# Five early weight tiles through PSUM banks, twelve instead of sixteen before the first block, and new nominal times for the planner of a fused attention and two-block MLP kernel

## The chip, the cores and the metric

The kernel runs on one core of a Trainium2 chip. The metric is device microseconds of one execution, taken as the median of several executions; less is better.

## The reference

Attention over 2 x 8 heads of 1152 keys, in which neighbouring pairs of queries are averaged first (576 pooled queries a head), then two MLP blocks over the 1152 resulting rows of 512. All arrays are float32.

```python
q_pool = q.reshape(B, H, S // 2, 2, D).mean(axis=3)        # B 2, H 8, S 1152, D 64
scores = np.matmul(q_pool, k.transpose(0, 1, 3, 2)) / np.sqrt(D)
attn = softmax(scores, axis=-1)
x = (attn @ v).transpose(0, 2, 1, 3).reshape(1152, 512)
h = x @ w_in                                               # 512 x 2048, first block
P = a[0] + a[1] * h + a[2] * h**2 + a[3] * h**3
Q = 1.0 + abs(b[0]) * abs(h) + abs(b[1]) * h**2
x = (P / (Q + 1e-06)) @ w_out                              # 2048 x 512
h = x @ w2_in                                              # second block
out = (np.maximum(h, 0) + np.log1p(np.exp(-np.abs(h)))) @ w2_out
```

## The kernel before

The two weight pairs of the MLP arrive as float64 bits. Each of the 64 weight tiles (128 x 512) is loaded as pairs of 32-bit words (`w_load`, a DMA of 512 KB on SP's queue into one of two buffers `wraw`) and decoded on the chip in five steps. In the attention part these are operations of their own, `w0` to `w4`: `w0` on ScalarE scales the high word into the tile `pk` (`w_abs`, L446), `w1` on VectorE shifts it left by three (`w_conv`, L452), `w2` on VectorE ors in bits of the low word (L458), `w3` on ScalarE copies it as the high half of the weight tile `w` (L954 in the attention part, L468 in the blocks), and `w4` on VectorE subtracts to get the low half (L396, `w<-pk,w`). `wl` is the load. In the second half of the work one more VectorE operation (L455) sets the sign. Products are made of high and low halves, three matmuls each.

The attention works through 8 pairs of heads (NP = 8; j = 0 to 7), each in 9 steps of query tiles by three column groups. A group's scores (L543, TensorE) go into a PSUM bank, VectorE takes the maximum (L550), ScalarE the exponential (L563, tile `p`), TensorE transposes (L514, tile `t`, another bank), ScalarE or GpSimd writes the rounded half (`ph`, L506, L613 and L623), VectorE or GpSimd the remainder (`pl`, L396), and TensorE multiplies by v (L643). Eight banks (NB = 8) serve all of these in turn; VectorE's and ScalarE's reads free them. The next pair's keys and queries are loaded, transposed, split (`khi`, `klo`, `qhi`, `qlo`; L783, L811, L816) and moved by DMAs on SP's queue (`dma_k`, `dma_q`, `dma_qd`, all L517) while a pair is worked. `dma_qd` copies parts of `qhi` and `qlo` into `qdh` and `qdl` (kind `dd`); `qhi` has one buffer, so the next pair's `qhi` (kind `qh0`) can't be written before those copies have read it.

The order of the whole attention part is written by a planner. Every operation has a kind and a nominal time: its base (nine units a pair) plus an offset of its kind from the table `O`, and corrections by step in the pair (`OT`) and for the first and last pair (`OJ`, `OU`). `op` adds these up; `run` sorts each engine's operations by nominal time and then issues them, always taking the engine whose head is ready first by a small model of durations. That fixes the instruction order of every engine and which bank each operation gets. `weight` makes the six operations of a weight tile.

Before the first block 16 tiles are decoded: three singly in pairs 2, 3 and 4 (NE = 3, pool `we`), and 13 around the last pair, into the space of two pools that are released then (`early` becomes `wra`, seven tiles; `even` becomes `wrb`, seven tiles).

The first block takes 48 units (24 groups of two, k = 0 to 23) of 24 matmuls up (L1054) and 24 down (L1103) for each pair of units; the activation takes 3 + 3 VectorE operations and one for the low half on 128 x 768 tiles in each group (L1077 to L1079, L1088 to L1090, L396). The remaining weight tiles are decoded meanwhile by `w_step`, which moves up to one tile each through split, convert, scale and load. `w_pace` calls it in every second unit at first (r0 = 50), later in two of five (r1 = 40), and `w_need` calls it as often as needed when a tile is wanted that isn't there. The tiles' order of use is `order`: index 0 to 15 for the first half of the first block, 16 to 31 for its second half, 32 to 63 for the second block. The second block (up L1135, down L1157) has 48 units too, with a step in nine of ten (r2 = 90), each issued after the unit's last ScalarE copy.

Of the kernel before, what the change touches and what calls it, by code (L numbers as in the profile page):

```python
# [10 lines left out]
I32 = mybir.dt.int32  # L11
# [22 lines left out]
    ne=3,  # L34
    r0=50,
    r1=40,
    r2=90,
    whd=0,
# [27 lines left out]
    "R": 2.6459,
    "U": 2.3672,
    "U1": 2.601,
    "U2": 2.8694,
    "X0": 4.1997,  # L70
    "X1": 4.539,
    "kq": -3.3775,
    "lv": 1.3594,
    "pq": 0.4094,
    "qt0": 0.6348,
    "qh0": 0.9195,
    "ql0": 1.4074,
    "qt1": 1.843,
    "qh1": 1.897,
    "ql1": 2.3854,  # L80
    "dq0": 2.0734,
    "dq1": 1.6718,
    "dd": 4.2928,
    "kt0": 4.4127,
    "kh0": 4.5969,
    "kl0": 5.3629,
    "kt1": 5.1134,
    "kh1": 5.4542,
    "kl1": 5.853,
# [31 lines left out]
    "P3": 1.2299,
    "P4": 1.4149,
    "P5": 2.1976,
    "P6": 1.5711,
    "P7": 1.8637,
    "P8": 1.9534,
}
OT = {
# [35 lines left out]
}  # L164
OJ = {
    "lv": (-1.2907, 0),
    "fa": (0.1493, 0),
    "fh": (1.1474, 0),
    "fp": (-2.3014, 0),
    "fl": (-0.1074, 0),  # L170
    "v0": (-0.2845, 0),
    "vw0": (-0.0476, 0),
    "v1": (1.894, 0),
    "vw1": (2.0223, 0),
    "S0": (-0.0354, -0.1233),
# [1177 lines left out]
```

## Time and profile before

| what | value |
|---|---|
| median of 3 runs | 713.07 us (712.73 to 715.3) |
| profiled execution, its own time | 711.51 us |
| span of the profiled execution | 709.4 us |
| TensorE busy | 681.0 us (96%) |
| VectorE busy | 556.5 us (78%) |
| ScalarE busy | 493.5 us (70%) |
| GpSimd busy | 207.3 us (29%) |
| first matmul of the first block | 298.1 us |
| first matmul of the second block | 496.5 us |

The span runs from the first to the last instruction; 2.1 us of the execution lie outside it. Busy times are sums over the whole span, in which the attention and the two blocks have different limits, so the engines are compared stretch by stretch. A busy TensorE is not TensorE at its peak: ends of matmuls are modelled and small waits between them can hide.

### The profile page before, as it was taken

What the parts mean: (1) busy time and instruction counts of PE and PEld (TensorE: products, weight loads), DVE (VectorE), ACT (ScalarE), POOL (GpSimd) and SP (SyncE); (2) the same over time, 40 slices, a digit from 0 to 9 for tenths busy, and PEclk for the clock granted to TensorE, in tenths of its full rate; (3) what the DMA queues carried; (4) which work ended last, traced back from release to release, by engine and by line L of the source; (5) the groups of instructions that cost most, each with busy time, mean ns of one, the idle gap of its engine ahead of it and who ended that gap; (6) DMA issues with size and microseconds to landing.
All of it is one profiled execution on the core that took longest, in us unless ns stands there. A gap on an engine that the chain in (4) does not pass through costs nothing.

```text
span 709.4 us, 11830 instructions
## 1 busy us (share of the span) xinstructions
PE 681.0 (96%) x4076; PEld 633.2 (89%) x4076; DVE 556.5 (78%) x1080; ACT 493.5 (70%) x1135; POOL 207.3 (29%) x357
## 2 busy tenths in 40 slices
PE   7998999999999987789999999999999999999997
PEld 6898999998999875689999999999999999999996
DVE  5987989999898899989999999999775775511122
ACT  4888999989999998778777677776544554422221
POOL 4876687777768545600000000000000000000000
PEclk9999999999999999999999999999999999999999
DMA  3383736464736643431221022210043342101011
GB/s 100 102 187 85 171 90 163 114 155 104 179 84 141 148 128 120 140 98 60 62 86 62 31 84 72 83 57 3 2 149 118 95 141 92 61 1 45 1 45 44
DMA packets 60395, 65.68 MB, mean 93 GB/s; under 512 B 21552, under 2 KB 49456, under 8 KB 60336
## 3 DMA queue, kind: packets, MB, share of 16 engines
q1 hardware_dynamic: 59152, 63.95, 33.5%
q10 hardware_dynamic: 1184, 0.98, 0.4%
q8 instruction: 32, 0.52, 0.3%
q14 instruction: 27, 0.22, 0.1%
HBM read 47.71 MB, written 2.36 MB: 71 GB/s over the span
## 4 chain that ended last, share of the span: by engine, by line
PE 62%; DVE 15%; ACT 13%; DMA 4%; issue 4%; SPq 1%; ACTq 0%; DVEq 0%
PE acc L1157 14%; PE h L1135 14%; PE t L514 8%; PE pv L643 8%; PE s L543 8%; PE acc L1103 5%; PE h L1054 5%; ACT p L563 4%; DMA wraw<-in_moe_w_in_dram 3%; DVE p L1077 2%; DVE m L1089 2%; DVE m L1079 2%; ACT ph L506 2%; DVE p L1088 1%; ACT c L613 1%
## 5 line engine op out<-in xcount | busy, mean ns | idle before, releaser
L563 ACT ACTIVATE p<-s,mb 128x384 f32<-128x384 f32 x216 | 125.4, 593 | 6.1 <-DVE mb L554 5.9
L550 DVE TENSOR_REDUCE nm<-s 128x1 f32<-128x384 f32 x216 | 111.7, 550 | 12.6 <-PE s L543 11.1
L396 DVE TENSOR_TENSOR gl<-p,gh 128x384 fp32r<-128x384 f32 (+1 forms) x72 | 49.6, 690 | 91.3 <-ACT gh L1144 90.0
L514 PE MATMUL t<-ident,p 128*128 128x128 f32 x648 | 102.0, 277 | 8.4 <-ACT p L563 6.1
L1054 PE MATMUL h<-xh,w 128*128 128x384 f32 x384 | 99.4, 338 | 3.5 <-DVE p L1078 2.5
L1143 ACT ACTIVATE p<-h 128x384 f32<-128x384 f32 x48 | 23.6, 492 | 108.8 <-PE h L1135 108.7
L1135 PE MATMUL h<-xh,w 128*128 128x384 f32 x384 | 98.4, 336 | 0.0
L514 PEld LDWEIGHTS t<-ident,p 128*128 128x128 f32 x648 | 78.8, 142 | 18.8 <-ACT p L563 12.2
L1103 PE MATMUL acc<-gh,w 128*128 128x384 f32 x384 | 92.9, 336 | 0.3 <-ACT gh L1064 0.2
L643 PE MATMUL pv<-ph,v 128*128 128x256 f32 (+1 forms) x288 | 90.9, 326 | 1.0 <-ACT p L563 0.5
L1157 PE MATMUL acc<-w,gh 128*128 128x512 f32 x288 | 89.5, 392 | 0.0
L396 DVE TENSOR_TENSOR pl<-t,ph 128x384 fp32r<-128x384 f32 (+1 forms) x160 | 78.6, 510 | 4.4 <-ACT ph L506 3.7
L643 PE MATMUL pv<-pl,v 128*64 128x256 f32 (+1 forms) x288 | 78.1, 299 | 1.8 <-POOL pl L396 0.5
L396 POOL TENSOR_TENSOR pl<-c,ph 128x384 fp32r<-128x384 f32 (+1 forms) x80 | 75.8, 952 | 5.1
L506 ACT CAST ph<-t 128x384 fp32r<-128x384 f32 (+1 forms) x160 | 70.8, 467 | 5.7 <-PE t L514 4.8
L1135 PEld LDWEIGHTS h<-xh,w 128*128 128x128 f32 x384 | 70.5, 188 | 4.3 <-ACT p L1143 0.4
L1054 PEld LDWEIGHTS h<-xh,w 128*128 128x128 f32 x384 | 70.1, 190 | 4.4 <-issue 4.3
L1103 PEld LDWEIGHTS acc<-gh,w 128*128 128x128 f32 x384 | 68.6, 188 | 1.6 <-ACT gh L1064 1.5
L1054 PE MATMUL h<-xl,w 128*128 128x384 f32 x192 | 64.8, 338 | 0.0
L1135 PE MATMUL h<-xl,w 128*128 128x384 f32 x192 | 64.7, 337 | 0.0
L1157 PEld LDWEIGHTS acc<-w,gh 128*128 128x128 f32 x288 | 53.4, 188 | 9.0
L1103 PE MATMUL acc<-gl,w 128*128 128x384 f32 x192 | 59.1, 335 | 0.0
(129 smaller groups left out, 1475.4 us busy)
## 6 DMA issues: line engine op xcount, KB each, us to landing
wraw<-in_moe_w_in_dram SPq DMA_DIRECT2D x32, 512.0 KB, 3.9
wraw<-in_moe_w_out_dram SPq DMA_DIRECT2D x32, 512.0 KB, 3.3
vr<-in_v_dram SPq DMA_DIRECT2D x8, 576.0 KB, 6.2
kr<-in_k_dram SPq DMA_DIRECT2D x15, 288.0 KB, 5.1
qr<-in_q_dram SPq DMA_DIRECT2D x15, 256.0 KB, 4.4
out_dram<-m SPq DMA_DIRECT2D x15, 128.0 KB, 1.7
ks1a<-khi SPq DMA_DIRECT2D x4, 288.0 KB, 3.2
ks1a<-klo SPq DMA_DIRECT2D x4, 288.0 KB, 4.0
```

The lines of the kernel that those rows point to most:

```text
L396: return eng.tensor_tensor(out=o, in0=a, in1=b, op=ALU.subtract)
L506: nc.scalar.copy(out=out, in_=in_)
L514: nc.tensor.transpose(o[0:rows, i * 128:i * 128 + n], a, ident[0:n, 0:n])
L543: nc.tensor.matmul(out=o, lhsT=p, rhs=r, start=(m == 0), stop=(m == len(l) - 1))
L550: op("M" + str(n % 3), "DVE", fn=lambda: nc.vector.tensor_reduce(out=NM[i][:, n:n + 1], in_=tl[k], axis=AX.X, op=ALU.max, negate=True), R= ...
L563: nc.scalar.activation(out=o, in_=tl[k], func=AF.Exp, bias=MB[i][:, t:t + 1], accum_out=DEN[i][:, n:n + 1])
L643: nc.tensor.matmul(out=o, lhsT=p, rhs=r[:, m, 0:w], start=(c == a == 0), stop=(c == C - 1 and a == 1))
L1054: nc.tensor.matmul(out=h, lhsT=w[:, wi, wd], rhs=x[:, d, xcols(c)], start=(n == 0), stop=(n == 3 * ND - 1))
L1103: nc.tensor.matmul(out=st["acc", c, d], lhsT=w[:, wi, wd], rhs=g, start=(first and n == 0), stop=(last and n == 2))
L1135: nc.tensor.matmul(out=h, lhsT=w[:, wi, d * 128:(d + 1) * 128], rhs=x[:, d, xcols(c)], start=(n == 0), stop=(n == len(mm) - 1))
L1143: nc.scalar.activation(out=p, in_=h, func=AF.Softplus)
L1157: nc.tensor.matmul(out=st["acc", c, t], lhsT=g[:, t * 128:(t + 1) * 128], rhs=w[:, wi], start=(first and n == 0), stop=(last and n == 2))
```

## The change

Five tiles instead of three are decoded singly, at base times 13.8, 23.1, 30.3, 39.7 and 47.7 (pairs 1 to 5), and seven instead of 13 around the last pair, at bases 61.5 to 67.1; the list `wt` holds all twelve. `pk` of these tiles is a PSUM bank out of the planner's eight instead of a tile in SBUF, and `w1`, `w2` and `w4` no longer count in the planner's model as holders of the port that VectorE and GpSimd share. `wrb` is not filled before the first block; its seven places go to the list `freed`, with two fewer of `wl_`. The first block's steps start at tile 12, not 16, and stop for its last six units (rq = 6). The tile `p` has five buffers, not six. All nominal times are new; corrections now exist by pair (0, 6, 7) and, for the first pair's preparation and the weight tiles, by operation (`OF`). `run` may look past a blocked head when all heads are blocked.

```diff
-    ne=3,
+    ne=5,
+    wt=(13.827, 23.117, 30.255, 39.714, 47.66, 61.48, 62.487, 63.019, 64.546, 64.568, 65.923, 67.055),
+    rq=6,
...
-    "kq": -3.3775,
+    "kq": -1.7841,
-    "dd": 4.2928,
+    "dd": 3.7605,
-    "qh0": 0.9195,
+    "qh0": 0.981,
...
-    "dd": (1.5635, 0),
+    ("dd", 0): 0.106,
...
-NB, NP_, NPH, NCP = 8, 6, 5, 2
+NB, NP_, NPH, NCP = 8, 5, 5, 2
...
-        if kind in OJ and not 0 < j < 7:
-            when += OJ[kind][j >= 7]
-        if kind in OU and not 0 < j < 7:
-            when += OU[kind][j >= 7][int(b - 9 * j)]
+        when += OJ.get((kind, j), 0) + OF.get((kind, round(b, 3)), 0)
+        if (kind, j) in OU:
+            when += OU[kind, j][int(b - 9 * j)]
...
+        def beyond(q):
+            for i in [i for i in q[1:] if i not in start][:40]:
+                x = ready(i)
+                if x:
+                    return x
...
-                a, i, bank = min(x for x in (ready(q[0]) for q in queue.values() if q) if x)
+                heads = [x for x in (ready(q[0]) for q in queue.values() if q) if x]
+                a, i, bank = min(heads or [x for x in (beyond(q) for q in queue.values() if q) if x])
...
-    def w_abs(i):
-        st["pk", i] = wst.tile([128, 512], I32, tag="pk", name="pk", bufs=3)
+    def w_abs(i, g=None):
+        st["pk", i] = wpk.tile([128, 512], I32, tag="pk", name="pk", bufs=3) if g is None else g.bitcast(I32)
...
-        raw, pk, w = ring("raw"), ring("pk"), ("W", i)
+        raw, pk, w = ring("raw"), ring("bk"), ("W", i)
-        op("w0", "ACT", fn=lambda: w_abs(i), R=[raw], W=[pk], new=[("pk", 3)], **act(512))
-        op("w1", "DVE", fn=lambda: w_conv(i, 0), R=[pk], W=[pk], port=True, ns=340, lat=150)
-        op("w2", "DVE", fn=lambda: w_conv(i, 2), R=[raw, pk], W=[pk], port=True, **dve(512))
+        op("w0", "ACT", fn=lambda: w_abs(i, bank(pk, "pk")), R=[raw], W=[pk], new=[("bk", NB)], **act(512))
+        op("w1", "DVE", fn=lambda: w_conv(i, 0), R=[pk], W=[pk], **dve(512))
+        op("w2", "DVE", fn=lambda: w_conv(i, 2), R=[raw, pk], W=[pk], **dve(512))
-        op("w4", "DVE", fn=fl, R=[pk, w], W=[w], port=True, **dve(512))
+        op("w4", "DVE", fn=fl, R=[pk, w], W=[w], **dve(512))
...
-        for i in range(NE):
-            at(9 * (i + 2) + T["pre0"], weight, i, ((lambda: we), []))
-        for n in range(NRA + NRB - 1):
-            a = n < NRA
-            at(te + T["ce"] + T["prea"] + n * T["pred"], weight, NE + n,
-               ((lambda: st["wra"]) if a else (lambda: st["wrb"]), [("wra",) if a else ("wrb",)]))
+        for i, t in enumerate(T["wt"]):
+            at(t, weight, i, ((lambda: we), []) if i < NE else ((lambda: st["wra"]), [("wra",)]) if i < NE + NRA
+               else ((lambda: st["wrb"]), [("wrb",)]))
...
-        freed = [st["wrb"]] + [wl_] * (NW - NP1 - NE - NRA - NRB)
-        n0 = NE + NRA + NRB - 1
+        freed = [st["wra"]] * max(0, NE + NRA - len(T["wt"]))
+        freed += [st["wrb"]] * min(NRB, NE + NRA + NRB - len(T["wt"]))
+        freed += [wl_] * (NW - NP1 - NE - NRA - NRB)
+        n0 = len(T["wt"])
...
-            if every(i, T["r0"] if i < NCH * FH else T["r1"]):
+            if i < NU - T["rq"] and every(i, T["r0"] if i < NCH * FH else T["r1"]):
```

## Rows read from the trace of the kernel before

**Rows 1.** The page's first part: busy time, share of the span, instructions of each engine.

```profile
PE 681.0 (96%) x4076; PEld 633.2 (89%) x4076; DVE 556.5 (78%) x1080; ACT 493.5 (70%) x1135; POOL 207.3 (29%) x357
```

**Rows 2.** Windows: pairs 1, 3, 5, 7, the two blocks; length, busy of five engines.

```profile
42.84:76.99 34.15, 32.35 (x225) 30.32 (x224) 27.70 (x72) 29.04 (x89) 23.13 (x42) 0.95 0.57 129
...
110.36:143.43 33.07, 32.88 (x236) 30.08 (x235) 30.14 (x78) 31.13 (x95) 25.24 (x44) 1.00 0.56 136
...
176.50:208.30 31.80, 31.66 (x232) 29.70 (x231) 28.82 (x74) 29.85 (x92) 24.22 (x44) 1.00 0.56 124
...
240.41:296.67 56.26, 43.94 (x278) 36.55 (x276) 52.76 (x119) 48.94 (x132) 29.10 (x45) 0.97 0.48 145
298.20:496.50 198.30, 195.56 (x1111) 193.87 (x1112) 192.56 (x250) 147.00 (x199) 1.71 (x3) 0.99 0.20 64
496.50:709.40 212.90, 208.91 (x1051) 188.87 (x1049) 100.63 (x177) 83.62 (x161) 0.00 (x0) 1.00 0.21 66
```

**Rows 3.** Windows of the tile pk alone, last pair: length, VectorE, ScalarE, clock, DMA.

```profile
240.41:296.67 56.26, 25.05 (x39) 17.45 (x27) 0.97 0.48 145
```

**Rows 4.** Groups of instructions on VectorE, last pair: busy and mean ns, idle before.

```profile
L396 DVE TENSOR_TENSOR pl<-t,ph 128x384 fp32r<-128x384 f32 x21 | 11.4, 549 | 0.1
L396 DVE TENSOR_TENSOR w<-pk,w 128x512 fp32r<-128x512 f32 x13 | 9.7, 747 | 0.1
L458 DVE SCALAR_TENSOR_TENSOR pk<-wraw,pk 128x512 int32<-128x512 int32 x13 | 9.3, 712 | 0.0
L452 DVE TENSOR_SCALAR pk<-pk 128x512 int32<-128x512 int32 x13 | 6.6, 509 | 2.3 <-ACT pk L446 2.3
```

**Rows 5.** Timeline of ScalarE, at the last pair's first weight tile: start, duration, idle before.

```profile
243.01 0.66 ACT L446 ACTIVATE pk<-wraw 128x512 f32<-128x512 f32 x1 [1.52 <-DMA wraw<-in_moe_w_in_dram]
```

**Rows 6.** Timeline of pair 1, queries' copies and the next pair's queries.

```profile
48.82 2.49 SPq L517 DMA_DIRECT2D qdh<-qhi  x2
...
54.00 0.49 ACT L811 ACTIVATE qhi<-t 128x384 fp32r<-128x384 f32 x1 [1.92 <-DMA qdh<-qhi]
...
55.14 0.55 PE L514 MATMUL t<-ident,p 128*128 128x128 f32 x3 [1.65 <-DVE qlo L816]
```

**Rows 7.** Timeline of pair 2, first and last step of its weight tile.

```profile
102.81 0.72 ACT L446 ACTIVATE pk<-wraw 128x512 f32<-128x512 f32 x1
...
108.90 0.68 DVE L396 TENSOR_TENSOR w<-pk,w 128x512 fp32r<-128x512 f32 x1
```

**Rows 8.** Groups of instructions on VectorE, first block: weight steps.

```profile
L458 DVE SCALAR_TENSOR_TENSOR pk<-wraw,pk 128x512 int32<-128x512 int32 x24 | 17.0, 710 | 0.3
L396 DVE TENSOR_TENSOR w<-pk,w 128x512 fp32r<-128x512 f32 x22 | 15.0, 687 | 0.1
L452 DVE TENSOR_SCALAR pk<-pk 128x512 int32<-128x512 int32 x23 | 9.8, 433 | 1.9 <-ACT pk L446 1.9
```

**Rows 9.** Timeline of VectorE, first block: last steps of weight tiles 1-2, 19, 20-21.

```profile
300.46 1.46 DVE L396 TENSOR_TENSOR w<-pk,w 128x512 fp32r<-128x512 f32 x2
...
438.71 0.69 DVE L396 TENSOR_TENSOR w<-pk,w 128x512 fp32r<-128x512 f32 x1
...
449.11 1.29 DVE L396 TENSOR_TENSOR w<-pk,w 128x512 fp32r<-128x512 f32 x2
```

**Rows 10.** Timeline at the second block's start: first down matmul, an up unit, weight tiles.

```profile
511.00 0.63 PE L1157 MATMUL acc<-w,gh 128*128 128x512 f32 x2
511.06 0.69 DVE L396 TENSOR_TENSOR w<-pk,w 128x512 fp32r<-128x512 f32 x1
...
513.08 0.51 PE L1135 MATMUL h<-xh,w 128*128 128x384 f32 x2
...
513.20 0.69 DVE L396 TENSOR_TENSOR w<-pk,w 128x512 fp32r<-128x512 f32 x1
...
515.19 0.63 PE L1157 MATMUL acc<-w,gh 128*128 128x512 f32 x2
...
516.98 0.69 DVE L396 TENSOR_TENSOR w<-pk,w 128x512 fp32r<-128x512 f32 x1
```

More of the change, by code (lines that the diff above doesn't have):

```diff
@@ L121 @@
[L121 to L126, printed above, removed]
+    "S0": -1.1791,
+    "S1": -1.1966,
+    "S2": -0.8221,
+    "M0": -0.913,
+    "M1": -0.9621,
+    "M2": -0.7136,
+    "B": -0.2834,
+    "E0": -0.1512,
+    "E1": -0.2925,
+    "E2": -0.083,
+    "T0": -0.1096,
+    "T1": -0.0187,
+    "T2": 0.3837,
+    "V0": 0.3574,
+    "V1": 0.47,
+    "V2": 0.1866,
+    "H0": 0.48,
+    "H1": -0.0415,
+    "H2": 0.7,
+    "L0": 0.9316,
+    "L1": 0.7,
@@ new lines @@
+    "L2": 0.852,
+    "D0": 0.8392,
+    "D1": 2.4795,
+    "R": 2.5969,
+    "U": 2.5174,
+    "U1": 2.5202,
+    "U2": 2.6796,
+    "X0": 3.6534,
+    "X1": 4.8093,
+    "kq": -1.7841,
+    "lv": 1.0305,
+    "pq": 0.0502,
+    "qt0": 0.6381,
+    "qh0": 0.981,
+    "ql0": 1.3317,
+    "qt1": 1.9406,
+    "qh1": 2.2316,
+    "ql1": 2.4744,
+    "dq0": 1.4222,
+    "dq1": 1.9804,
+    "dd": 3.7605,
+    "kt0": 4.288,
+    "kh0": 4.9547,
+    "kl0": 5.0536,
+    "kt1": 4.8793,
+    "kh1": 5.9619,
@@ new lines @@
+    "kl1": 6.0298,
+    "kt2": 4.8162,
+    "kh2": 5.3835,
+    "kl2": 5.7135,
+    "dk0": 5.0813,
+    "dk1": 7.9856,
+    "v0": 5.2568,
+    "v1": 3.7532,
+    "w0": -0.8043,
+    "w1": -0.3834,
+    "w2": 0.0952,
+    "w3": 0.6873,
+    "w4": 0.9189,
+    "wl": -4.3069,
+    "W0": 0.36,
+    "Y0": 0.36,
+    "N0": 0.53,
+    "W1": 0.358,
+    "Y1": 0.47,
+    "N1": 0.8012,
+    "W2": 0.58,
+    "Y2": 0.58,
+    "N2": 0.75,
+    "ft": 0.4933,
+    "vw0": 7.4376,
+    "vw1": 4.4384,
+    "fh": -0.4564,
@@ new lines @@
+    ("B", 0): -0.2858,
+    ("E0", 0): -0.3025,
+    ("T0", 0): -0.2217,
+    ("V0", 0): -0.0408,
+    ("L0", 0): 0.2981,
+    ("E1", 0): 0.0914,
+    ("T1", 0): -0.2528,
+    ("W1", 0): 0.1,
+    ("H1", 0): -0.5885,
+    ("N1", 0): -0.4899,
+    ("E2", 0): -0.1292,
+    ("T2", 0): -0.0427,
+    ("V2", 0): 0.1292,
+    ("L2", 0): 0.5367,
+    ("P0", 0): 0.0665,
+    ("P1", 0): 0.0827,
+    ("P2", 0): -0.1492,
+    ("P3", 0): 0.3185,
+    ("P4", 0): -0.1777,
+    ("P5", 0): -0.0624,
+    ("P6", 0): -0.5693,
@@ new lines @@
+    ("P2", 7): 1.6179,
+    ("P3", 7): 0.362,
+    ("P4", 7): 0.1335,
+    ("P5", 7): 0.0374,
+    ("P6", 7): 0.5144,
+    ("P7", 7): 0.5091,
+    ("P8", 7): 0.2714,
+    ("D0", 7): 0.4516,
+    ("D1", 7): 1.5645,
+    ("R", 7): 0.6009,
+    ("U", 7): 0.0407,
+    ("U1", 7): 0.6286,
+    ("U2", 7): 0.3967,
+    ("X0", 7): 0.9406,
+    ("X1", 7): 1.1654,
+}
+OF = {
+    ("fa", -8.5): 1.9317,
+    ("ft", -8.5): -0.7383,
+    ("fh", -8.5): 1.2958,
+    ("fp", -8.5): -2.0047,
+    ("fl", -8.5): -2.1025,
+    ("ft", -8.4): 0.193,
+    ("fh", -8.4): 2.4338,
+    ("fl", -8.4): 0.3248,
+    ("ft", -8.3): -0.1546,
+    ("fh", -8.3): 1.6391,
+    ("fl", -8.3): -0.5891,
+    ("ft", -8.2): -0.5138,
+    ("fh", -8.2): 3.0463,
+    ("fl", -8.2): 2.5087,
+    ("fa", -5): 1.2905,
+    ("ft", -5): -0.5085,
+    ("fh", -5): -0.4723,
+    ("fp", -5): -4.1843,
+    ("fl", -5): -1.357,
+    ("fa", 0.62): 0.0296,
+    ("ft", 0.62): -0.1528,
+    ("fh", 0.62): 1.0091,
+    ("fp", 0.62): -3.8952,
+    ("fl", 0.62): -0.4144,
+    ("ft", 0.92): -0.0483,
+    ("fh", 0.92): 1.232,
+    ("fl", 0.92): -0.6316,
+    ("ft", 1.22): -0.7034,
+    ("fh", 1.22): 0.5385,
+    ("fl", 1.22): -0.9915,
+    ("ft", 1.52): -0.7345,
+    ("fh", 1.52): 1.4228,
+    ("fl", 1.52): -0.3111,
+    ("fa", 1.82): 0.1252,
+    ("ft", 1.82): 0.3411,
+    ("fh", 1.82): 1.3348,
+    ("fp", 1.82): -1.477,
+    ("fl", 1.82): -1.0127,
+    ("wl", 13.827): -0.5629,
+    ("w0", 13.827): 0.855,
+    ("w1", 13.827): 0.2104,
+    ("w2", 13.827): -0.037,
+    ("w3", 13.827): -0.2527,
+    ("w4", 13.827): 0.2836,
+    ("wl", 23.117): -0.2785,
+    ("w0", 23.117): -0.5302,
+    ("w1", 23.117): 0.0512,
+    ("w2", 23.117): -0.3812,
+    ("w3", 23.117): -0.5989,
+    ("w4", 23.117): -0.0929,
+    ("wl", 30.255): 1.0986,
+    ("w0", 30.255): 0.4086,
+    ("w1", 30.255): 0.2865,
+    ("w2", 30.255): -0.0347,
+    ("w3", 30.255): -0.2956,
+    ("w4", 30.255): 0.4912,
+    ("wl", 39.714): 1.9066,
+    ("w0", 39.714): -0.2897,
+    ("w1", 39.714): -0.5172,
+    ("w2", 39.714): -0.8558,
+    ("w3", 39.714): -0.5999,
+    ("w4", 39.714): 0.4068,
+    ("wl", 47.66): 0.7309,
+    ("w0", 47.66): -0.514,
+    ("w1", 47.66): 0.3247,
+    ("w2", 47.66): 0.2417,
+    ("w3", 47.66): -0.0045,
+    ("w4", 47.66): 0.568,
+    ("wl", 61.48): 0.5054,
+    ("w0", 61.48): 0.5381,
+    ("w1", 61.48): 0.3569,
+    ("w2", 61.48): 0.066,
+    ("w3", 61.48): -0.2176,
+    ("w4", 61.48): -0.1587,
+    ("wl", 62.487): 3.1579,
+    ("w0", 62.487): 0.4494,
+    ("w1", 62.487): 0.324,
+    ("w2", 62.487): 0.0411,
+    ("w3", 62.487): -0.6088,
+    ("w4", 62.487): -0.5163,
+    ("wl", 63.019): 3.3362,
+    ("w0", 63.019): 0.3574,
+    ("w1", 63.019): 0.7662,
+    ("w2", 63.019): 0.3346,
+    ("w3", 63.019): 0.4578,
+    ("w4", 63.019): 0.6546,
+    ("wl", 64.546): 2.8556,
+    ("w0", 64.546): -0.0633,
+    ("w1", 64.546): 0.7127,
+    ("w2", 64.546): 0.3943,
+    ("w3", 64.546): 0.2142,
+    ("w4", 64.546): 0.2798,
+    ("wl", 64.568): 2.9918,
+    ("w0", 64.568): 1.3557,
+    ("w1", 64.568): 1.0115,
+    ("w2", 64.568): 0.5989,
+    ("w3", 64.568): 1.375,
+    ("w4", 64.568): 0.0852,
+    ("wl", 65.923): 2.4528,
+    ("w0", 65.923): 0.7778,
+    ("w1", 65.923): 0.3446,
+    ("w2", 65.923): 0.4945,
+    ("w3", 65.923): 0.7278,
+    ("w4", 65.923): 1.1846,
+    ("wl", 67.055): 3.0335,
+    ("w0", 67.055): 0.794,
+    ("w1", 67.055): 0.3483,
+    ("w2", 67.055): -0.0341,
+    ("w3", 67.055): 3.3686,
+    ("w4", 67.055): 0.4494,
@@ L322, in op @@
         b = st["t"]
-        j = int(b // 9)
+        j = max(0, int(b // 9))
         when = b + O.get(kind, 0)
@@ L1315, in attn_moe_kernel @@
         ap.release()
+        wpk.release()
         pa_.release()
```

258 lines of the change are left out of this document (107 added, 151 removed), and 175 rows, old and new, of tables (OT, OU).

## The prediction

> **What bounds the kernel now.** I read the page's first part first [rows 1]: TensorE is busy for 681.0 of 709.4 us, so at most 28 us are idle, and a change that removes no matmul can win only there or in waits too small to show. The windows by stretch say where they are [rows 2]. (A pair runs here from one last reciprocal to the next.) Pair 5, which decodes no weight tile, takes 31.80 us with TensorE busy for 31.66; pair 3, which decodes one, takes 33.07 with 32.88 (pairs 2 and 4 are like it). The last pair takes 56.26 us with TensorE busy for 43.94: 12.3 us idle (278 matmuls are on record against pair 5's 232, since its window holds the tail that other pairs overlap with the next). There VectorE is busy for 52.76 us, 94%, ScalarE for 48.94, 87%. In the first block VectorE (192.56 of 198.30 us) and TensorE (195.56) are level; in the second VectorE needs 100.63 of 212.90.
>
> So the last pair is bound by VectorE, and the windows of one tile say why: work on `pk` holds VectorE for 25.05 us there, 39 operations for 13 tiles, 1.93 us a tile [rows 3]. Without it VectorE would have 52.76 - 25.05 = 27.7 us to do, less than pair 5's 28.82. The groups [rows 4] show the three steps at 509, 712 and 747 ns, against 433, 710 and 687 in the first block, where GpSimd has nothing to do [rows 8].
>
> **The change part by part.** The sum is made against the profiled execution's 711.51 us, which is 1.56 below the median of 713.07; 1.56 is added at the end.
>
> *Six tiles fewer in the last pair.* What remains is 27.7 us and seven tiles. A tile's new price is not in the trace, since `pk` was never in a bank. Nearest are `w2` and `w4` themselves, 0.71 and 0.69 us for 512 columns [rows 8], and the remainder out of a bank, 0.549 us for 384 columns [rows 4], 0.73 for 512 if scaled by columns. I take 0.70 for each of the three steps, 2.1 a tile: `w1` loses its 0.43, the stalls of the other two go. That makes 27.7 + 14.7 = 42.4 us of VectorE, and at the same 94% busy a pair of 45.2 us: 11.0 less. Bounds: with all steps at the first block's prices (1.83 a tile) 43.2 us, 13.1 less; at 2.2 a tile 46.0; with VectorE only as busy as in pair 5 (28.82 of 31.80, 91%) 46.8, 9.5 less. ScalarE follows: its 27 steps on `pk` take 17.45 us [rows 3], 1.3 a tile, so six fewer bring its 48.94 us to 41, still below VectorE.
>
> One rule speaks against this part. The row shows `w1` at 433 ns undisturbed, well below `w2` at 710 for the same 512 columns [rows 8]. The Trainium skill, VectorE: DVE Perf Modes, section Why PSUM operands drop a tier, says that a PSUM operand takes away the mode that reads one tensor through both SBUF ports, and that 32-bit data then goes at the plain rate. By the row alone seven tiles would cost 12.8 us of VectorE, by the rule nearer the 14.7 I took: some 2 us on the pair. No run shown so far has `w1` in a bank.
>
> *Two tiles more in pairs 1 and 5.* A pair with a tile is 33.07 - 31.80 = 1.27 us longer [rows 2]; two make +2.5. Below: nothing, since VectorE idles for 2.9 us in pair 3; above: the whole 2 x 2.1 = 4.2. The dearer `w1` of all five (5 x 0.27 = 1.3) I cost at nothing, hidden by the same 2.9 us; without that cover it is +1.3.
>
> *The wait of pair 1.* Pair 1 takes 34.15 us without any tile, 2.35 more than pair 5. Its timeline shows one cause [rows 6]: `qhi` of pair 2 waits 1.92 us on ScalarE for the copies into `qdh`, issued at 48.82 behind the keys' copies on SP's queue; VectorE and then TensorE wait with it, TensorE 1.65. In the old tables these copies stand at 4 + 4.293 + 1.564 = 9.86 units and the waiting `qhi` at 9 + 0.92 = 9.92; in the new at 4 + 3.761 + 0.106 = 7.87 and 9.98. Two units are some 7 us, so the wait should go: -1.7 (0 to -2.35). The loads of the pair after next (`kq`, now at 9 - 1.78) are still ahead of the copies on SP's queue, five issues, which may eat into that margin.
>
> *The earlier loads at the last pair.* ScalarE waits 1.52 us for the first of the 13 tiles to land [rows 5], while the last pair's copies queue. By the tables the first of them is now loaded at 61.48 - 4.307 + 0.505 = 57.7 units, before at 61.8 - 2.92 = 58.9, so some 4 us earlier. That wait is inside the 56.26 us and counted there.
>
> *All other nominal times.* The same instructions in another order, with one buffer of `p` fewer. I take 0. Bounds: pairs 1 to 5 down to TensorE's 31.7, 5 x 1.4 = -7; the other way I allow the same.
>
> *Four more tiles in the first block.* It needs tiles 0 to 31 by the down matmuls of group 17, with 12 present instead of 16: 20 to decode. Counted through `w_pace`, 16 steps come in time and `w_need` forces four (two at k = 15, one each at 16 and 17). A group is 198.3 / 24 = 8.26 us, so group 17's down falls 17.5 x 8.26 = 145 us after the block's start, 442.7 in the old times. By then the old kernel had finished 19 tiles (the 19th at 438.71, the next two at 449.11) [rows 9], with VectorE 97% busy: one is lacking, at 0.71 + 0.69 + 0.43 = 1.83 us. I take +1.5; below 0, above four whole tiles, +7.3. From k = 21 on no paced steps are left, so VectorE gets that back too late for TensorE.
>
> *The start of the second block.* Its first down needs tile 36. The old kernel had it at 450 [rows 9], 61 us early. Counting steps, the new one enters the block with 34 tiles split, not 38, and splits 34, 35 and 36 after the first units' copies. The old trace does such steps at 511.06, 513.20 and 516.98, while the first down starts at 511.00 [rows 10]: a wait of up to 6. Up units of 2.1 us each (513.08 to 515.19) can go ahead, two of them without more buffers, 4.2 us. I take +1.5; bounds 0 and +6. VectorE has room for the rest of the four tiles (100.63 of 212.90).
>
> Sum: -11.0 + 2.5 - 1.7 + 1.5 + 1.5 = -7.2; 711.51 - 7.2 = 704.3, and with 1.56 **705.9 us**, 1.0% less. Half a per cent, 3.6 us, is about what a measurement of this kernel tells from no change: faster is below 709.5, slower above 716.6.
>
> **The rivals.**
>
> *The blocks take it back.* The first block's VectorE really pays all four tiles, or the second block's start waits its 6 us. For it: VectorE's 97%. Against: steps there run well ahead of their place (61 us), so they fill holes. First block alone: 705.9 + 5.8 = 711.7; second start alone: 705.9 + 4.5 = 710.4.
>
> *The last pair does not shrink so far.* Its waits may be a chain, scores to maximum to exponential to transpose, rather than VectorE's sum. For it: TensorE idles for 12.3 us there, and no row says that it is for VectorE alone. Against: VectorE's 94%. With half the gain: 705.9 + 5.5 = 711.4; the change then does not do what it says.
>
> *The new order is better throughout.* Pairs 1 to 5 near TensorE's 31.7 us: up to -7, 699.
>
> *Banks run short: slower.* A tile held `pk` from 102.81 to 109.58, 6.8 us [rows 7]. In a bank that leaves seven of eight for 12 x 6.8 = 81 us; if the attention is short of banks and slows to 7/8, it needs 81/7 = 11.6 us more: 705.9 + 11.6 = 717.5. It decides from a hold of about 6.3 us up and only if all eight banks are needed. Against: the planner opens a bank only when one is free and orders around it; with one or no tile at a time most of a pair has all eight.
>
> **How the numbers follow.** Forecast, 702.5 to 709.5: 0.45. Better order, below 702.5: 0.19. Blocks take it back: 0.18. Half the gain: 0.10. Banks: 0.08. The range from 699 to 713 leaves about 0.08 above and 0.08 below. Faster 0.45 + 0.19 = 0.64; same 0.18 + 0.10 = 0.28; slower 0.08. The likeliest case's own range is 702.5 to 709.5.
>
> **What would show it.** The last pair near 45 us with VectorE over 90% busy and `w1` near 0.7 us; pairs 2 to 4 near 33, 1 and 5 too; no wait of `qhi` for `qdh`; the first block starting about 10 us earlier and not much longer; the first down of the second block within 2 us of its third up unit. Wrong it would be if TensorE waited for `pk` banks in pairs 1 to 5, if `h` waited for VectorE around groups 15 to 17, or if tile 36 came late by the whole 6 us.

## The result, and the profile after

The changed kernel takes 705.3 us (median of 5 runs, 704.43 to 705.52) beside 713.07 for the kernel before on the same chip (712.14 to 715.3): a ratio of 0.9881 of the means (the medians give 0.9891), 95% interval 0.9861 to 0.9901. The forecast was 705.9. Its profiled execution took 705.37 us, with a span of 703.5 us. The number came out; most of the reason given for it did not.

The page's first part of the changed kernel answers to [rows 1]:

```profile
PE 682.0 (97%) x4076; PEld 630.0 (90%) x4076; DVE 558.7 (79%) x1082; ACT 494.3 (70%) x1135; POOL 196.8 (28%) x357
```

TensorE and VectorE were saved no work: they are busy 1 and 2 us longer (GpSimd, busy for 28% of the span, 10.5 us less). The 5.9 us that the span lost come out of TensorE's idle time. The windows of pairs 1, 3 and 5, the last pair and the two blocks answer to [rows 2] (length; busy of TensorE, its weight load, VectorE, ScalarE, GpSimd; granted clock; DMA share; GB/s). A correction to the prediction's wording: the mark that ends a pair in these windows is the third of its four reciprocals, not the last, here as there, so the last window holds the rest of pair 6 too.

```profile
43.83:74.37 30.54, 30.17 (x216) 27.32 (x215) 27.93 (x71) 29.25 (x89) 22.89 (x42) 1.00 0.50 114
...
107.63:140.84 33.21, 32.85 (x237) 30.16 (x236) 30.54 (x77) 31.25 (x96) 23.92 (x44) 1.00 0.58 134
...
173.96:207.97 34.01, 33.03 (x235) 29.77 (x234) 30.80 (x77) 31.24 (x96) 24.05 (x44) 1.00 0.57 132
...
240.19:289.57 49.38, 42.88 (x271) 36.53 (x270) 43.48 (x102) 41.35 (x117) 23.86 (x46) 0.93 0.26 82
290.60:490.00 199.40, 195.60 (x1115) 192.34 (x1113) 192.98 (x251) 148.68 (x201) 1.81 (x2) 1.00 0.20 64
490.00:703.50 213.50, 209.15 (x1050) 188.48 (x1048) 109.19 (x193) 88.14 (x169) 0.00 (x0) 1.00 0.24 76
```

Against [rows 2] the last pair is 6.88 us shorter and pair 1 is 3.61 shorter, although it now decodes a tile. Pair 5 is 2.21 longer, the blocks 1.10 and 0.60 longer. What is left of the 5.9 us is +0.99 up to pair 1's start, +0.19 over pairs 2 to 4 and 6, and -0.50 between the last pair and the first block. The mark between pairs 0 and 1 moves by itself: in the first run below, whose edit changes nothing before the last pair, pair 1 takes 32.31 us and ends at 77.02 (76.99 in the kernel before). Counted up to the end of pair 1, the changed kernel is 2.62 us ahead.

The weight steps in the last pair, windows of the tile pk and VectorE's groups, answer to [rows 3, 4]:

```profile
240.19:289.57 49.38, 14.39 (x21) 8.47 (x14) 0.93 0.26 82
```

```profile
L663 DVE TENSOR_SCALAR pk<-pk 128x512 int32<-128x512 int32 x7 | 4.8, 691 | 0.0
L669 DVE SCALAR_TENSOR_TENSOR pk<-wraw,pk 128x512 int32<-128x512 int32 x7 | 4.8, 687 | 0.0
L607 DVE TENSOR_TENSOR w<-pk,w 128x512 fp32r<-128x512 f32 x7 | 4.8, 680 | 0.0
```

The reader is to see two things. A tile from a bank takes VectorE 2.06 us, as the prediction took (2.1): `w1` rises from 433 ns undisturbed [rows 8] to 691, so the rule it cited (the Trainium skill, VectorE: DVE Perf Modes, section Why PSUM operands drop a tier) and the trace agree. VectorE's load in the last pair, 43.48 us, is near the forecast's 42.4. But the pair takes 49.38 us, not 45.2: VectorE is busy 88% of it, not 94%.

Cut in two at the last pair's own first reciprocal, the window shows why one share for all of it misleads. First the kernel before, then the changed one:

```profile
240.41:268.35 27.94, 22.89 (x153) 19.59 (x151) 25.97 (x62) 24.52 (x68) 12.82 (x21) 1.00 0.57 162
268.35:296.67 28.32, 21.05 (x125) 16.95 (x125) 26.78 (x58) 24.42 (x66) 16.28 (x24) 0.94 0.39 129
```

```profile
240.19:271.73 31.54, 25.51 (x161) 20.38 (x159) 31.08 (x71) 28.30 (x79) 14.51 (x27) 0.97 0.36 111
271.73:289.57 17.84, 17.37 (x110) 16.15 (x111) 12.39 (x33) 13.05 (x39) 9.35 (x19) 0.85 0.08 30
```

Before, VectorE is nearly full in both parts. In the changed kernel it is full in the first, 31.08 of 31.54 us, and in the second TensorE is, 17.37 of 17.84 us, at a granted clock of 0.85.

### The profile page after: what moved, and what is told of

Its sections match the earlier page's. It is cut to its first block, busy times and chain, and to the rows that moved or that the text cites. A ratio compares the mean times of both kernels' runs of the same rounds, so it can differ in the third digit from the quotient of the medians.

```text
span 703.5 us, 11809 instructions
## 1 busy us (share of the span) xinstructions
PE 682.0 (97%) x4076; PEld 630.0 (90%) x4076; DVE 558.7 (79%) x1082; ACT 494.3 (70%) x1135; POOL 196.8 (28%) x357
## 4 chain that ended last, share of the span: by engine, by line
PE 47%; DVE 6%; ACT 4%; DMA 3%; issue 1%; DVEq 0%; ACTq 0%; SPq 0%
PE acc L1365 13%; PE h L1343 12%; PE acc L1311 10%; PE h L1262 10%; DMA wraw<-in_moe_w_in_dram 2%; DMA wraw<-in_moe_w_out_dram 1%; PE pv L854 1%; PE t L725 1%; DVE m L1297 1%; ACT s L1292 1%; DVE p L1296 1%; ACT s L1291 1%; DVE m L1287 1%; DVE p L1285 1%; DVE pk L669 0%
## 5 line engine op out<-in xcount | busy, mean ns | idle before, releaser
L854 PE MATMUL pv<-pl,v 128*64 128x256 f32 (+1 forms) x288 | 76.6, 296 | 0.0
L607 POOL TENSOR_TENSOR pl<-c,ph 128x384 fp32r<-128x384 f32 (+1 forms) x80 | 73.5, 926 | 3.2
L717 ACT CAST ph<-t 128x384 fp32r<-128x384 f32 (+1 forms) x160 | 69.1, 466 | 7.5 <-PE t L725 6.0
```

The lines of the kernel that those rows point to most:

```text
L607: return eng.tensor_tensor(out=o, in0=a, in1=b, op=ALU.subtract)
L717: nc.scalar.copy(out=out, in_=in_)
L854: nc.tensor.matmul(out=o, lhsT=p, rhs=r[:, m, 0:w], start=(c == a == 0), stop=(c == C - 1 and a == 1))
```

## The experiments

Two theories stood at the start. Load: VectorE's sum sets the last pair, so six tiles fewer shorten it whatever the order. Banks: a tile in a bank takes something from the attention that the old order cannot spare, and the new nominal times are there to pay for it.

**Fewer tiles alone.** The kernel before, with twelve tiles ahead of the first block instead of sixteen (three in pairs, nine at the last pair), from SBUF, other times untouched.

```diff
-        for n in range(NRA + NRB - 1):
+        for n in range(9):
...
-        freed = [st["wrb"]] + [wl_] * (NW - NP1 - NE - NRA - NRB)
-        n0 = NE + NRA + NRB - 1
+        freed = [st["wrb"]] * 5 + [wl_] * (NW - NP1 - NE - NRA - NRB)
+        n0 = NE + 9
```

> The kernel before with its own nominal times and pk in SBUF, but nine tiles instead of 13 around the last pair (three single ones as before), so twelve ahead of the first block, whose steps start at tile 12. If the gain is VectorE's load in the last pair: four tiles at 1.93 us off it, 7.7 us, 8.2 of the pair at 94% busy, against some 1.7 us that the blocks give back in the changed kernel: 713.1 - 6.5 = 706.6, last window near 48 us. If the gain comes from the new nominal times or from the banks: 711 to 715, since neither is here.

711.29 us, ratio 0.9977 (0.9965 to 0.9989). The last pair fell by 2.07 us, not by 8. The window, and the groups of the tile pk inside it, say that the test was not pure: two tiles of the first block slipped forward into the pair (L468 is their rounding step).

```profile
240.65:294.84 54.19, 43.70 (x273) 37.35 (x272) 48.63 (x113) 46.27 (x127) 25.96 (x44) 0.94 0.44 134
```

```profile
L954 ACT CAST w<-pk x9: 617/623/638, 247.5 to 282.1; 128x512 fp32r<-128x512 f32 x9
L468 ACT CAST w<-pk x2: 621/622/622, 287.3 to 293.2; 128x512 fp32r<-128x512 f32 x2
```

**The changed kernel with the old nominal times.** Banks and twelve tiles as changed; the tables of the kernel before, tiles at about its places.

```diff
-    wt=(13.827, 23.117, 30.255, 39.714, 47.66, 61.48, 62.487, 63.019, 64.546, 64.568, 65.923, 67.055),
+    wt=(15, 24, 33, 42, 51, 61.8, 62.6, 63.4, 64.2, 65.0, 65.8, 66.6),
...
-    ("dd", 0): 0.106,
+    "dd": (1.5635, 0),
```

> The changed kernel (five tiles singly, seven around the last pair, banks, five buffers of p, no paced steps in the first block's last six units) with the nominal times of before; tiles at bases 15, 24, 33, 42, 51 and 61.8 to 66.6. By the load theory nearly the whole gain stays and only the wait of the next pair's queries for their copies comes back, about 2 us: 707.3. If the new times made the gain: 712 or more.

729.55 us, ratio 1.022 (1.02 to 1.0241): the load theory's 707.3 was wrong by 22 us. The other case, 712 or more, came true, but 18 us above its bound: the new times are worth 24 us once banks are used. The last pair, and one bank's story in it (timeline: start, length, idle before and its releaser):

```profile
247.56:312.91 65.35, 51.61 (x273) 42.67 (x272) 44.48 (x101) 42.17 (x118) 22.48 (x44) 0.82 0.26 79
```

```profile
270.05 0.64 ACT L455 ACTIVATE pk<-wraw 128x512 f32<-128x512 f32 x1
...
286.40 0.67 DVE L405 TENSOR_TENSOR w<-pk,w 128x512 fp32r<-128x512 f32 x1
...
287.13 0.69 PE L552 MATMUL s<-ks1b,qq1b 128*128 128x384 f32 x1 [1.57 <-DVE w L405]
```

The fifth late tile takes its bank at 270.05 and gives it back at 287.07, and scores have waited 1.57 us for it. The granted clock of the pair is 0.82, beside 0.97 [rows 2]. From first step to last the seven tiles hold banks for 85.8 us together, 12.3 each; in the changed kernel the same sums are 47.0 and 6.7. There, no row of TensorE's waits from pair 1 to the end of the last pair names a tile's step.

**Sixteen tiles through banks, old times.** The run before with three tiles in pairs and thirteen at the last pair, and the sixth buffer of `p` and the paced steps of the first block's last six units back.

```diff
-    ne=5,
-    wt=(15, 24, 33, 42, 51, 61.8, 62.6, 63.4, 64.2, 65.0, 65.8, 66.6),
+    ne=3,
+    wt=(24, 33, 42, 61.8, 62.6, 63.4, 64.2, 65.0, 65.8, 66.6, 67.4, 68.2, 69.0, 69.8, 70.6, 71.4),
...
-    rq=6,
+    rq=0,
...
-NB, NP_, NPH, NCP = 8, 5, 5, 2
+NB, NP_, NPH, NCP = 8, 6, 5, 2
```

> The kernel before with its own nominal times, three single tiles, 13 around the last pair and sixteen ahead, only that pk of these tiles lies in PSUM banks (and the planner may look past blocked heads). By the load theory VectorE's three steps cost 2.06 us a tile instead of 1.93: 13 x 0.13 = 1.7 us more, 714.8. If the banks made the gain, by freeing GpSimd and VectorE of each other: 709 or less. If banks run short in the last pair: 718 or more.

738.59 us, ratio 1.0345 (1.0321 to 1.0369): against load, and as the case of short banks had it (718 or more), by 20 us more. The last pair takes 80.01 us with VectorE busy for 69% of it.

```profile
242.95:322.96 80.01, 58.68 (x278) 47.24 (x276) 55.23 (x120) 49.08 (x130) 22.95 (x46) 0.77 0.33 102
```

**Sixteen tiles under the new times.** The changed kernel with four more tiles at its end.

```diff
-    ... 65.923, 67.055),
+    ... 65.923, 67.055, 67.8, 68.5, 69.2, 69.9),
```

> The changed kernel with its new nominal times and four tiles more at the end of the last pair (bases 67.8, 68.5, 69.2, 69.9), so sixteen ahead again. By the load theory VectorE gets 4 x 2.06 = 8.2 us more in the last pair, some of it in holes that VectorE has there now (5.9 us idle), and the blocks get back up to 1.7: 705.3 + 8.2 - 1.7 = 711.8, not below 708. If order or banks made the gain: 704 to 706.

725.49 us, ratio 1.0159 (1.0139 to 1.0178). Neither case foresaw it; four tiles cost 20 us, where their VectorE work is 8.2. The last pair's waits show why (who waits for whom, total us, times, longest): a transpose stands for 5.7 us until a tile's last step frees a bank. The new times carry the tiles they were laid for, and not four more.

```profile
PE t L725 <- DVE w L607: 7.1, 2, 5.7
```

**No tile in pairs 1 and 5.** The changed kernel with ten tiles ahead.

```diff
-    ne=5,
+    ne=3,
-    wt=(13.827, 23.117, 30.255, 39.714, 47.66, 61.48, ...
+    wt=(23.117, 30.255, 39.714, 61.48, ...
```

> The changed kernel without the tiles of pairs 1 and 5: ten tiles ahead of the first block, three in pairs 2 to 4 and seven in the last pair, all through PSUM banks, the other nominal times as changed. If a tile in a pair costs what its steps take there and the first block, whose VectorE is busy 192.98 of 199.40 us, must decode the two itself at 1.83 us each: pairs 1 and 5 shorter by 2.5 us together, first block longer by 3.7, so about 706.5. If the tiles of pairs 1 and 5 hide under TensorE's work: no gain in the pairs, about 709. If they cost more than their steps, by the banks that they hold (pair 5 had grown by 2.2 us): 704 or less.

706.69 us, ratio 0.9923 (0.9892 to 0.9954), as its first case said, though its parts were smaller (1.8 us off the two pairs, not 2.5; 2.6 on the block, not 3.7). Pair 1 takes 30.13 us without its tile (30.54 with it), pair 5 32.60 (34.01), the first block 202.00 (199.40). So pair 1's gain is the order's, and its tile costs 0.4 at most (without it pair 1 begins 0.54 later and ends at 74.50, not 74.37); pair 5's costs 1.4 and the other 0.8 is the order's; two tiles fewer ahead cost the block 2.6.

**The same with `pk` in SBUF.**

```diff
-        op("w0", "ACT", fn=lambda: w_abs(i, bank(pk, "pk")), ..., new=[("bk", NB)], **act(512))
+        op("w0", "ACT", fn=lambda: w_abs(i, wst.tile([128, 512], F32, tag="pk", name="pk", bufs=3)), ..., new=[("pk", 3)], **act(512))
```

> The kernel of the run before with the scratch tile pk in SBUF, three buffers, as before the change, instead of a PSUM bank; order and tiles the same. It tells the banks from the order. If the banks cost under the new times too (under the old ones they cost 17 us and more): 3 us or more faster than with the banks. If the new times are laid so that the banks are free when TensorE wants them: within 1.5 us of it, since the three VectorE steps take 1.97 us from SBUF and 2.06 us from a bank. If the banks are the gain (GpSimd and VectorE no longer in each other's way): 2 us or more slower.

724.09 us, ratio 1.0169 (1.0133 to 1.0205). Its third case (2 us or more slower) came true, but it tells less than hoped: its last pair (63.9 us) holds twelve tiles, since five of the first block slipped forward through the free buffers. The next three runs avoid that.

**Place and times, one against the other.** Eleven tiles, four in pairs 1 to 4 and seven at the last pair. First the changed kernel without pair 5's tile:

```diff
-    ne=5,
+    ne=4,
-    wt=(..., 39.714, 47.66, 61.48, ...
+    wt=(..., 39.714, 61.48, ...
```

> The changed kernel without the tile of pair 5: eleven ahead of the first block, four in pairs 1 to 4 and seven in the last pair, through banks; the measure for the next two runs. If that tile costs pair 5 the 2.2 us that it had grown by and the block decodes it for 1.8 us: 705, within 0.7 of the changed kernel. If the block has it for nothing: 703.3.

706.73 us, ratio 0.9909 (0.9883 to 0.9934); neither case, 705 or 703.3, was met. Pair 5 became 1.36 us shorter (32.65) and the first block 2.40 longer (201.80).

Then `pk` in two SBUF buffers of the attention, and two for the blocks in a pool of their own (where the changed kernel has three); `w1`, `w2` and `w4` count as holders of the port in the planner's model again:

```diff
-        op("w0", "ACT", fn=lambda: w_abs(i, bank(pk, "pk")), ..., new=[("bk", NB)], **act(512))
+        op("w0", "ACT", fn=lambda: w_abs(i, wst.tile([128, 512], F32, tag="pk", name="pk", bufs=2)), ..., new=[("pk", 2)], **act(512))
...
-        op("w4", "DVE", fn=fl, R=[pk, w], W=[w], **dve(512))
+        op("w4", "DVE", fn=fl, R=[pk, w], W=[w], port=True, **dve(512))
```

> The run before with pk of the eleven tiles in SBUF, two buffers, and the blocks' scratch in a pool of its own as in the changed kernel (so that no tile of the block can slip into the last pair, as five did in the ten-tile kernel from SBUF and two in the twelve-tile kernel with the old times). Same tiles, same nominal times. If banks by themselves cost, and the new times only pay for it: faster than with banks, 702 or less. If the times fit the banks and nothing else differs but the steps (1.97 against 2.06 us a tile): within 1.5 us. If the two buffers or the shared port hold the tiles up: 3 us or more slower.

And the same under the tables of the kernel before (five buffers of `p`, and no paced step in the last six units, as changed):

```diff
-    wt=(13.827, 23.117, 30.255, 39.714, 61.48, 62.487, 63.019, 64.546, 64.568, 65.923, 67.055),
+    wt=(15, 24, 33, 42, 61.8, 62.6, 63.4, 64.2, 65.0, 65.8, 66.6),
```

> The run before with the nominal times of the kernel before: four tiles in pairs 1 to 4, seven from step 61.8 at a distance of 0.8, from SBUF. With the run of the old times through banks (729.6) it tells what banks cost under the old times, and with the run before what the new times are worth without banks. If fewer tiles in the last pair were worth 8 us by VectorE's load, as forecast, and the times nothing: 706. If the old times keep the pair long whatever its load: 711. If the old times alone cost what the run through banks lost: 725 or more.

| last pair of seven tiles | old times | new times |
|---|---|---|
| `pk` in SBUF, 11 tiles | 713.93 us, 1.0005 (0.9988 to 1.0023) | 716.13 us, 1.0026 (1.0009 to 1.0044) |
| `pk` in banks, 11 tiles | not run | 706.73 us, 0.9909 (0.9883 to 0.9934) |
| `pk` in banks, 12 tiles | 729.55 us, 1.022 (1.02 to 1.0241) | 705.3 us, 0.9881 (0.9861 to 0.9901) |

The case of two buffers or the port holding the tiles up (3 us or more slower) came true for the new times from SBUF; the old times from SBUF came nearest to the case of a pair kept long whatever its load (711). The windows of the last pair: old times from SBUF, new times from SBUF, new times from banks.

```profile
239.86:293.11 53.25, 42.70 (x273) 36.10 (x272) 42.14 (x101) 41.75 (x118) 24.36 (x44) 0.97 0.33 97
```

```profile
240.08:295.38 55.30, 44.14 (x271) 37.23 (x270) 44.80 (x101) 42.15 (x117) 26.11 (x46) 0.94 0.24 73
```

```profile
238.85:287.51 48.66, 41.71 (x271) 35.55 (x270) 43.55 (x101) 41.41 (x117) 23.94 (x46) 0.96 0.26 83
```

Neither half of the change is worth anything here by itself (the first run, with fewer tiles, gained 0.2%): fewer tiles with the old times give 3 us in the last pair and lose 2.5 in the first block (200.80 us) and 1.3 in the second; new times without banks gain nothing; banks without new times lose 16. In the first window VectorE's load is what the forecast wanted, 42.14 us, and it is busy for 79% only. Cut at the pair's first reciprocal as above, and with VectorE's longest wait:

```profile
239.86:269.72 29.86, 23.53 (x153) 19.62 (x151) 26.28 (x62) 23.48 (x65) 12.67 (x21) 1.00 0.52 150
269.72:293.11 23.39, 19.17 (x120) 16.48 (x121) 15.86 (x40) 18.27 (x53) 11.69 (x23) 0.93 0.09 30
```

```profile
DVE pk L461 <- ACT pk L455: 3.8, 4, 1.6
```

The seven tiles stand where the first seven of the thirteen stood, so up to the first reciprocal VectorE has the same 62 operations as before and nothing is gained (29.86 us, before 27.94). All the work that went, 10.92 us of VectorE, went from the second part, which became 4.93 us shorter: there no engine is full, VectorE is busy for 68% and TensorE for 82%. In the whole pair VectorE's waits that the profile names are 9.9 us, beside 3.1 before, most for ScalarE (3.8 for `w0`). The reading is that the old places and order hold the pair open. It is not pure: this run also has five buffers of `p`, not six, and two of `pk`, not three, which were not tested alone; one `w0` waits 1.28 us for `w4` to give back a buffer of `pk`.

Why the new times do not suit SBUF is seen in the second kernel's timeline, 17 us into its last pair:

```profile
257.44 0.79 POOL L607 TENSOR_TENSOR xl<-xs,xh 128x288 fp32r<-128x288 f32 x1
257.47 1.31 DVE L607 TENSOR_TENSOR w<-pk,w 128x512 fp32r<-128x512 f32 x1 [2.17 <-ACT w L1165]
258.19 1.45 POOL L607 TENSOR_TENSOR pl<-c,ph 128x384 fp32r<-128x384 f32 x1
...
259.41 0.58 ACT L774 ACTIVATE p<-s,mb 128x384 f32<-128x384 f32 x1 [1.58 <-DVE mb L765]
...
260.13 0.44 PE L725 MATMUL t<-ident,p 128*128 128x128 f32 x2 [2.76 <-ACT p L774]
```

`w4` waits 2.17 us for `w3`, which the planner has put later on ScalarE, and then takes 1.31 us, overlapping GpSimd's `xl` and then its `pl`, which takes 1.45 us; in the run with banks `w4` and `pl` take 0.68 and 1.01. The maximum behind them is late, then the exponential, and TensorE stands 2.76 us, where the run with banks has 0.69. How much of the 9.4 us is the stretched steps and how much the two buffers and the planner's other order was not separated.

**One bank fewer, no tile in any.** The kernel before with seven banks.

```diff
-NB, NP_, NPH, NCP = 8, 6, 5, 2
+NB, NP_, NPH, NCP = 7, 6, 5, 2
```

> The kernel before with seven PSUM banks for the attention, not eight; the eighth lies idle, and pk stays in SBUF. A tile through a bank holds it from 5 to 10 us, so in the last pair one bank or more is gone most of the time. If the shortage of banks is what made the old times through banks 17 us dearer: the last pair, at 56.26 us, grows by 5 us or more, and the other pairs too; in all 725 or more. If one bank can be spared and the loss was of another kind (the order of the steps): within 3 us of 713.

739.02 us, ratio 1.0372 (1.0331 to 1.0413). Pair 3 takes 36.36 us [rows 2: 33.07], of which TensorE idles for 1.52 instead of 0.19 and is on record as busy for 1.96 more at a full clock (small waits between matmuls can hide in that); the last pair 64.58 [rows 2: 56.26].

```profile
121.26:157.62 36.36, 34.84 (x236) 29.96 (x235) 30.64 (x77) 31.95 (x95) 25.21 (x44) 1.00 0.54 123
264.32:328.90 64.58, 51.30 (x280) 41.38 (x278) 52.73 (x119) 49.54 (x132) 27.83 (x45) 0.87 0.44 126
```

So a bank that is missing costs time by itself, in an order that the planner lays anew for seven: 25 us in all by the medians, 3.3 in pair 3. The last pair's 8.3 us is an upper figure, read in an execution of 744.63 us, 5.6 above the median, at a granted clock of 0.87. The old times through banks had 85.8 / 65.35 = 1.3 banks gone on average; how much of their loss is waits for banks and how much goes with the lower clock, 0.82, was not separated.

**The wait of pair 1 alone.** The kernel before with one nominal time changed.

```diff
-    "dd": (1.5635, 0),
+    "dd": (-0.4, 0),
```

> The kernel before with one nominal time changed, the correction of the first pair for dd, the write of qdh, from 1.5635 to -0.4, so that its transfer starts earlier and ScalarE's load of qhi need not wait 1.52 us. If that wait was on the path: 1.7 us faster, 711.4 beside 713.07. If other work of that stretch sets the pair's end: no change, 713.0.

713.83 us, ratio 1.0015 (0.9995 to 1.0035): no change, as the second case said (the 1.52 us in the text above is the wait of [rows 5]; the one meant is 1.92 [rows 6]). Yet pair 1 took 31.86 us instead of 34.15, and the last pair began 2.04 us early. The profile shows where that went in its execution. Windows of 4 us early in the last pair, first of the kernel before, then of this one:

```profile
244.00:248.00 4.00, 2.90 (x19) 2.52 (x19) 4.00 (x12) 3.86 (x12) 0.61 (x3) 1.00 0.88 202
248.00:252.00 4.00, 2.75 (x20) 2.23 (x20) 3.82 (x8) 3.97 (x12) 2.15 (x3) 1.00 0.61 192
252.00:256.00 4.00, 3.08 (x21) 2.75 (x22) 4.00 (x11) 3.54 (x12) 1.14 (x2) 1.00 0.15 29
```

```profile
244.00:248.00 4.00, 1.96 (x14) 1.35 (x13) 3.41 (x9) 3.44 (x9) 1.06 (x3) 1.00 0.67 164
248.00:252.00 4.00, 3.28 (x17) 2.88 (x16) 3.75 (x10) 3.34 (x10) 1.25 (x2) 0.56 0.40 135
252.00:256.00 4.00, 4.00 (x20) 4.00 (x20) 2.68 (x7) 2.58 (x9) 2.27 (x3) 0.59 0.42 133
```

TensorE was busy for 1.96 of 4 us, not 2.90; then the granted clock stood near its lower level (1.2 of 2.4 GHz) for some 7 us, VectorE idled for the slower scores, and by 268.47 the lead was gone (268.35 in the kernel before). That is one execution; that the gain does not arrive, the median of ten says.

**More matmuls where TensorE idles.** The changed kernel with added work: fifteen small matmuls of zeros, which nothing reads.

```diff
+        for t in (66.2, 66.43, 66.65, 66.85, 66.97):
+            at(t, warm, 3)
```

> The changed kernel with fifteen more matmuls of zeros, three at each of five points of the last pair where TensorE had stood idle for about half the time (266 to 272 us), which nothing reads: added work. If the granted clock of 0.50 from 270 to 277 us is owed to that idling and costs the pair time: the clock stays near 1.00, the last window falls from 49.38 to about 47 us and the whole to 703. If VectorE sets the end there and the clock costs nothing: 705.3. If the added matmuls only stand in TensorE's way or take banks: up to 707.

706.75 us, ratio 0.992 (0.9893 to 0.9947). The third case, up to 707, fits. From 264 to 279 us the changed kernel's clock, then this one's, and then that of the run without pair 5's tile, which has no added matmuls, at the same place of its pair:

```profile
264.00:279.00 15.00, 12.41 (x64) 10.45 (x62) 11.76 (x29) 11.06 (x32) 5.65 (x12) 0.77 0.21 73
```

```profile
264.00:279.00 15.00, 12.69 (x73) 10.05 (x72) 10.96 (x27) 10.33 (x30) 4.56 (x9) 0.89 0.25 83
```

```profile
262.68:277.68 15.00, 12.01 (x69) 10.20 (x68) 12.40 (x31) 11.82 (x34) 6.42 (x13) 0.89 0.22 75
```

The time did not fall: from pair 6's last reciprocal to the last pair's first this kernel lost 1.69 us (19.60 instead of 17.91), and up to the second it won 0.75 (8.18 instead of 8.93). The 0.75 can't be put down to the fill, nor the clock of 0.89: the run without added matmuls has the same 8.18 us and 0.89 in its execution, and over the four executions of this kernel the mean clock was 0.994 to 0.997, over the five of the changed one 0.993 to 0.997. So the fill gained nothing, and that it raised the clock is not shown. No run beat the changed kernel.

## Why the number was right and the reason was not

| step of the prediction | forecast, us | measured, us |
|---|---|---|
| last pair, six tiles fewer | -11.0 | -6.88 |
| pair 1: tile and `qhi` wait | +1.27 - 1.7 | -3.61 |
| pair 5: tile | +1.27 | +2.21 |
| other nominal times | 0 | +0.68 outside pairs 1, 5 and 7 |
| first block, one tile lacking | +1.5 | +1.10 |
| start of the second block | +1.5 | +0.60 |
| sum | -7.2 | -5.90 |

**The step that failed is the last pair's**: that VectorE's load, at 94% busy, bounds all of it, and that the order, taken at 0, is free. The load was forecast well (42.4 us; 42.14 from SBUF, 43.48 from banks). But with that load and the old order the pair takes 53.25 us, and with the new order VectorE bounds only the first 31.5 us, and TensorE the last 17.8. Part of the missing 4.1 us goes with the clock: from 271.73 to 280.66 us TensorE is busy for 8.73 of 8.93 us at a granted clock of 0.71, where the run without pair 5's tile takes 8.18 us at 0.79. How large that part is was not separated. The rival that named this, waits in a chain and half the gain, had a chance of 0.10 and was nearer: the pair gave 63% of the forecast's 11.0, and with the old order 27%. The 94% that I held against it belonged to thirteen tiles. It did not say what else would bound the pair once tiles were gone: under the old order 10.92 us less of VectorE's work made the second part 4.93 us shorter, and the first no shorter.

**The order's 0 was wrong with banks in the sum.** Under the old times the same tiles through banks cost 729.55 us; the new times bring that to 705.3. Part of the -3.61 us of pair 1 is theirs too: its tile costs 0.4 by the run without it.

**The banks rival was right in its mechanism, and wrong in where it ends.** It said that banks are scarce and priced that at 11.6 us; one bank gone costs 25 us in the whole, and the tiles' banks under the old times came with 16. It does not show in the changed kernel: in the last pair the new times hold a bank for 6.7 us a tile and not 12.3. The price was not a matter of the hold's length alone, as I had worked it out: in pairs 1 to 5 the five tiles hold theirs for 7.8 to 12.9 us, longer than the 6.8 taken [rows 7] and than the 6.3 from which it was to decide. Yet pairs 2 to 4 take what they took before (33.26, 33.21 and 33.12 us beside 33.37, 33.07 and 33.07), and pair 5's tile costs 1.4, near the 1.27 of a tile from SBUF. Under the new times those pairs could spare a bank for 8 to 13 of their 33 us; under the old ones pairs 2 to 4 took 33.88 us each with a hold of 7.4.

**The `qhi` wait** is gone, and pair 1 is shorter, as stated. But by itself that gain does not reach the end (713.83 beside 713.11), so -1.7 is not shown to be a term of its own.

**Pairs 1 and 5**: 1.27 us for a tile stood well for pair 5 (1.4 by the run without it) and not for pair 1 (0.4 at most). `w1`'s extra 0.27 was hidden, as taken, as far as pair 3 shows: 33.21 us beside 33.07.

**The blocks** took back 1.70 us of the 3.0 forecast. The first block's 1.10 is not clear of the spread: the same block, unchanged, takes 199.3 and 200.3 us in the kernels before with one earlier transfer and with seven banks, beside 198.3 [rows 2]. VectorE does not pay for four tiles there either: it is busy for 192.98 us in 251 operations, before for 192.56 in 250 [rows 2]. The four are decoded in the second block, where VectorE's work grows by 16 operations and 8.56 us. That a tile too few costs the first block time is seen with eleven and ten tiles ahead, 201.80 and 202.00 us. At the second block the third and fourth up units went ahead, as the step had it: the last of its first three tiles came at 508.53 and the first down at 508.66.

Two errors made the total right: 4.1 us too much in the last pair against 3.2 too little in pair 1. That they cancel is luck. A third helped: the sum for the profiled execution was 704.3 and it took 705.37, but the 1.56 us added for the median had no counterpart after, where the median, 705.3, is 0.07 below the profiled time.

## What to carry to other kernels

Where every engine works through a queue laid out by hand, a stage's busy share does not tell what taking work away is worth: measure removal under the old order first, since it may be nothing (713.93 beside 714.01), and cut the stage into parts, since each may have a bound of its own (VectorE for 31.5 us, then TensorE for 17.8). A scratch tile moved into PSUM costs bank time, its hold from first step to last; before trusting such a move, run the kernel with one bank fewer and see what that costs. Edits whose gain needs each other (here the times and the banks) have no price each, and the mixed cases do not bound the whole: each half alone gave 713 to 730 us, both together 705.3.

## What the runs showed of the hardware that was not expected

In the kernel with the one earlier transfer, TensorE was busy 1.96 of 4 us in one window of the last pair; then the granted clock was 0.56 and 0.59 in the next two windows of 4 us, and the lead of 2 us that pair 1 had gained was lost by 268.47, in that one execution. The changed kernel has such a stretch too (0.71 from 271.73 to 280.66 us). Executions of one kernel differ with it: without pair 5's tile, one with a mean clock of 1.000 took 705.78 us, one at 0.997 took 706.23, and two at 0.994 took 707.60 and 709.37.
